# Bucket attention with two feed-forward stages: bucket bits of later pairs in four products per half, and a reordered prologue

## The chip, the cores and the metric

One core of one Trainium2 chip runs the whole program. The metric is the device time of one execution in microseconds (us); lower is better.

## The reference

```python
def _attn_ref(q, k, v, proj):                     # q, k, v: (2, 8, 768, 64), proj: (64, 6)
    q_bits = (np.einsum('bhsd,dk->bhsk', q, proj) > 0).astype(np.int64)
    k_bits = (np.einsum('bhsd,dk->bhsk', k, proj) > 0).astype(np.int64)
    q_bucket = np.sum(q_bits * powers, axis=-1)
    k_bucket = np.sum(k_bits * powers, axis=-1)
    mask = q_bucket[:, :, :, None] == k_bucket[:, :, None, :]
    scores = np.where(mask, scale * np.matmul(q, k.transpose(0, 1, 3, 2)), -1000000000.0)
    scores = scores - np.max(scores, axis=-1, keepdims=True)
    attn = np.exp(scores)
    attn = attn / (np.sum(attn, axis=-1, keepdims=True) + 1e-09)
    return np.matmul(attn, v)
```

The attention's rows (1536 tokens of 512) then go through a mixture of eight experts, of which each token takes one, and through a dense layer with an ELU between two products. The change touches the attention alone.

## The kernel before, in words

There are 16 heads (two batches of eight). Two heads make a **pair**, so there are eight pairs; a head has 768 queries, and 128 of them make a **tile**, so a pair has 12 tiles and the main loop runs over 96 tiles, numbered through. A **half** is 384 of the 768 columns. Every float32 value that goes into a product is split into a rounded part ("hi") and the rest ("lo"), and the products of the parts are added up.

**Operands of the scores.** A head has four arrays: `qa` and `ka` hold hi and lo rows, `qb` and `kb` hold the missing cross term and, from row 64 on, the bucket bits of queries and keys, coded with a huge constant `BIG` so that a pair of different buckets falls far below every other score. There are four sets of these arrays (`st` 0 to 3), two pairs' worth: while one pair is worked on, the next one's are filled.

**Preparing a pair** takes six steps (`prep`, L580): four times `prep_T` (TensorE turns half of the queries or keys, tile `prep`; ScalarE rounds it to hi, VectorE takes lo) and twice `prep_Z` (the bits of a half, tile `zps`). A half of bits is six products in `prep_Zm` (L229): hi, lo and hi again of the queries against rounded weights, the same rounded weights and the weights' rest, then the same for the keys; `prep_Ze` (L245) compares with zero and scales, on VectorE. `restack` (L266) moves the finished rows by DMA from the SP queue to the place where the products want them: six moves of 192 KB for the queries of a pair, six for the keys, six small ones for the bits. In a pair's tiles the steps are issued after tiles 1, 2, 4, 5, 7 and 8, for the next pair.

**A tile** goes through: S (four score products, L314 and L315, into one of two PSUM buffers), M (VectorE's maximum, L333, then two small operations on GpSimd, L334 and L335), E (ScalarE's exponential, L342), T (six transposes, L362, each half rounded by ScalarE, L364, and its rest taken by VectorE, L365), V (four value products per tile, L378) and, for every three tiles, O (the sums of a half, copied by ScalarE, moved by DMA and added by GpSimd, L388) and R (the joining product `sp`, L454, with its two VectorE evictions, L462 and L481). The loop issues tile n's S beside tile n-1's M and E, tile n-3's T and an earlier V. The order on every engine is the order in which the code issues; each engine and the SP queue work strictly in that order. Three PSUM buffers (`ps_t`) serve T, preparation, bits and R.

**The prologue** fills pair 0: its first head's bits are put in place by VectorE without a DMA (`first_Ze`, L238). GpSimd clears constant rows (`constant_rows`), clears and fills `rw` and `rw_end`, the joining weights, and copies a half of the keys. `keep_warm` issues products whose result nobody reads.

Of the kernel before, what the change touches and what calls it, by code (L numbers as in the profile page):

```python
# [8 lines left out]
F32 = mybir.dt.float32  # L9
# [11 lines left out]
NBITS = 6  # L21
# [4 lines left out]
def kernel(  # L26
# [129 lines left out]
        for nm in ("qa", "qb", "ka", "kb"):  # L156
            opnd[st, nm] = ap1.tile([128, S], F32R, name=f"{nm}{st}")

    def constant_rows(st):
        nc.gpsimd.memset(opnd[st, "qb"][64:96].bitcast(F32), 0.0)  # L160
        nc.gpsimd.memset(opnd[st, "qb"][96:96 + NBITS].bitcast(F32), 1.0)
        nc.gpsimd.memset(opnd[st, "kb"][64:96].bitcast(F32), -BIG)

    constant_rows(1)
    bdf, bdh, bdl = (ap1.tile([128, 2, 128], t, name="bd" + x) for x, t in (("f", F32), ("h", F32R), ("l", F32R)))
    nc.vector.memset(bdf, 0.0)
    for hh in range(2):
        rows = slice(64 * hh, 64 * hh + 64)
        src = pj[rows, None, :].to_broadcast([64, 2, NBITS])
        for nm, g0, c0, step in ((0, 32 * hh, 0, NBITS), (1, 64, NBITS * hh, 32)):  # L170
            dst = bdf[rows, nm, g0:g0 + 2 * step].rearrange("p (r c) -> p r c", r=2)[:, :, c0:c0 + NBITS]
            nc.scalar.activation(dst, src, AF.Copy)
    nc.scalar.activation(bdh, bdf, AF.Copy)
    nc.vector.tensor_tensor(bdl, bdf, bdh, ALU.subtract)
    bd = {nm: (bdh[:, i], bdl[:, i]) for i, nm in enumerate("qk")}
    amp = ap1.tile([128, 1], F32, name="amp")
    thr = ap1.tile([128, 1], F32, name="thr")
# [4 lines left out]
        nc.vector.memset(amp[p0:p0 + n], a)  # L182
        nc.vector.memset(thr[p0:p0 + n], t)

    nc.gpsimd.memset(rw, 0.0)
    for hh in range(2):
        p0 = 64 * hh
        rows, idc = slice(p0, p0 + 64), ident[p0:p0 + 64, None, p0:p0 + 64]
        nc.gpsimd.tensor_copy(rw[rows, :, hh, 0:D], idc.to_broadcast([64, H // 2, D]))
        nc.gpsimd.tensor_copy(rw_end[rows, :, 0:D], idc.to_broadcast([64, 2, D]))  # L190
    nc.gpsimd.memset(zt0, 0.0)

    hl = {}

# [52 lines left out]
        )  # L247

    def prep_Z(pr, j):
        prep_Zm(pr, j, "q")  # L250
        prep_Zm(pr, j, "k")

        def evac():
            prep_Ze(pr, j)
            if j == 1 and pr:
                restack(pr, "z")

        return (lambda: None), evac

    def restack(pr, what, heads=(0, 1)):  # L260
        for hh in heads:
            st = 2 * (pr % 2) + hh
            r0 = 64 * hh

            def cp(dst, p0, src, s0, n):
                nc.sync.dma_start(  # L266
                    opnd[st, dst][p0:p0 + n].bitcast(F32), src[s0:s0 + n].bitcast(F32)
                )

            if what == "q":  # L270
                hi, lo = hl[pr, "q"]
                cp("qa", 0, hi, r0, 64)
                cp("qa", 64, lo, r0, 64)
                cp("qb", 0, hi, r0, 64)
            elif what == "k":
                hi, lo = hl[pr, "k"]
                cp("ka", 0, hi, r0, 64)
                cp("ka", 64, hi, r0, 64)
                cp("kb", 0, lo, r0, 64)
            else:  # L280
                cp("kb", 64, zt[pr], (64, 96 + NBITS)[hh], NBITS)
                cp("kb", 96, zt[pr], (96, 64 + NBITS)[hh], NBITS)
                cp("qb", 64, zt[pr], 32 * hh, 2 * NBITS)

    vst = {}

# [103 lines left out]
    def stage_O(m):  # L390
# [2 lines left out]
        r0 = 64 * hh  # L393
        ps = ops.pop(m)
        if pr == NPAIR - 1 or hh == 0:
            t = ap2.tile([128, HC], F32, tag="osb", name="osb", bufs=2)
            osb.setdefault((pr, hf), []).append(t)
        if pr == NPAIR - 1:
            nc.scalar.activation(t, ps, AF.Copy)  # L399
# [2 lines left out]
        if m >= NM - 6:  # L402
            nc.scalar.activation(t, ps[0:64], AF.Copy)
            early.append(lambda: nc.vector.tensor_tensor(t, ps[64:128], t, ALU.add))
        else:
            w, u = (raw_p.tile([128, PW], F32, tag="w", name=x)[:, 0:HC] for x in ("o2", "o1"))
            nc.scalar.activation(w, ps, AF.Copy)
            nc.sync.dma_start(u[r0:r0 + 64], w[64 - r0:128 - r0])
            add.append((3 * m + 11, t, w[r0:r0 + 64], u[r0:r0 + 64]))

    rinv = {}
    sums_m = {}
# [179 lines left out]
    keep_warm(15)  # L592
    for j in range(2):
        both(prep_T(0, "q", j))
    restack(0, "q", (0,))
    for j in range(2):
        both(prep_T(0, "k", j))
    khi, klo = hl[0, "k"]
    nc.scalar.activation(opnd[0, "ka"][0:64], khi[0:64], AF.Copy)
    nc.gpsimd.tensor_copy(opnd[0, "ka"][64:128], khi[0:64])  # L600
    nc.scalar.activation(opnd[0, "kb"][0:64], klo[0:64], AF.Copy)
    for st in (2, 3):
        constant_rows(st)
    for j in range(2):
        prep_Zm(0, j, "q")
    for j in range(2):
# [2 lines left out]
        if j == 0:  # L609
            first_Ze(0, "q", 0, 128)  # L610
    first_Ze(0, "q", 128, HC)
    first_Ze(1, "q")
    load_pair(0, "v")
    load_pair(1, "k")
    for what in ("q", "k"):
        restack(0, what, (1,))

    def load_gates(hh, end):
        rows = slice(64 * hh, 64 * hh + 64)
# [19 lines left out]
    for b in range(B - 1):  # L639
        n0 = per * (b + 1) + HALF + 7  # L640
        for hf in range(2):
# [5 lines left out]
                    at(i, f)  # L647

            at(n0 + 8 * hf, start)
    for j in range(2):  # L650
        at(1, prep_Ze, 0, j)
    at(1, restack, 0, "z", (1,))
    for i in range(6):
        at(1 + i, prep_V, 0, i // 3, i % 3)
    for hh in range(2):
        at(9 + 3 * hh, load_gates, hh, False)
        at(61 + 3 * hh, load_gates, hh, True)
# [225 lines left out]
    for n in range(NQ + 3):  # L883
# [16 lines left out]
            late[0]()  # L900
        if n < NQ:
            stage_S(n)
        m, part = divmod(n - 13, HALF)
        if 0 <= m < NM - 3 and part == 0:
            early.append(stage_R(m))
        if n == NQ:
            stage_R(NM - 3)()
        m, part = divmod(n - 6, HALF)
# [14 lines left out]
            split_piece(0, nc.gpsimd, nc.gpsimd, rest0)  # L923
            xt0 = [raw_p.tile([128, KD * CAP], F32R, tag="w", name="xt0") for _ in range(2)]
        if nx < NPAIR:
            if s % 3 and s < 9:
                late = prep(nx, s // 3 * 2 + s % 3 - 1)
            if s in v_at:
                i = v_at.index(s)
                early.append(lambda a=(nx, i // 3, i % 3): prep_V(*a))  # L930
# [428 lines left out]
```

## Time and profile before

| | |
|---|---|
| median of 3 runs | 722.96 us (722.31 to 724.34) |
| the profiled execution: its time, its span | 723.3 us, 721.5 us |
| mean granted clock of TensorE | 0.993 |
| busy: TensorE / its weight loads | 704.7 us (98%) / 633.3 us (88%) |
| busy: VectorE / ScalarE / GpSimd | 553.6 (77%) / 422.7 (59%) / 206.0 us (29%) |
| attention (tiles 0 to 95) | from about 11 to about 255 us of the span |

Busy time of an engine says where it worked, not what held the others up. The chain that ended last follows the work back from the end, at each step to what released it; the timelines list what an engine did in order, with the idle time before an instruction and what ended it. [...]

### The profile page before, as it was taken

To read this page: it belongs to the slowest core of one execution; us is meant where nothing else is said; L and a number is where in the kernel's file an instruction comes from. 1 tells how busy PE (TensorE), PEld (TensorE's weight loads), DVE (VectorE), ACT (ScalarE), POOL (GpSimd) and SP (SyncE) were. 2 spreads that over 40 slices of the span, in tenths; PEclk is the share of its full clock that TensorE was granted. 3 is DMA by queue.
4 is the path that set the end of the run, shared out by engine and by line. 5 is a ranking of instruction groups with operands and counts; after the bars stand their busy time and mean duration, and the time that the engine had idled before them with its cause. 6 is when DMAs were issued, how large, how long until landed. Compare 5 with 4: busy or idle time off the path is not lost.

```text
span 721.5 us, 12243 instructions
## 1 busy us (share of the span) xinstructions
PE 704.7 (98%) x4239; PEld 633.3 (88%) x4240; DVE 553.6 (77%) x1045; ACT 422.7 (59%) x843; POOL 206.0 (29%) x491
## 2 busy tenths in 40 slices
PE   6999999999999999999999999999999999999996
PEld 4899999999999988999999999788888888888885
DVE  5888988989898988788888887977688546934333
ACT  3887978879788875666666675444543224422221
POOL 7445454455545554112352241000000000002012
PEclk9899999999999999999999999999999999999999
DMA  8747576585773137987889786332122000001011
GB/s 192 181 104 172 163 184 173 129 213 137 167 218 98 76 105 224 291 251 222 260 241 251 203 230 191 103 102 84 63 88 87 31 0 2 1 0 59 0 59 61
DMA packets 108532, 97.69 MB, mean 135 GB/s; under 512 B 33416, under 2 KB 94472, under 8 KB 108464
## 3 DMA queue, kind: packets, MB, share of 16 engines
q1 hardware_dynamic: 106000, 90.44, 46.8%
q0 software_dynamic: 2304, 6.40, 2.4%
q8 instruction: 35, 0.57, 0.3%
q14 instruction: 33, 0.27, 0.1%
q10 hardware_dynamic: 160, 0.00, 0.0%
HBM read 64.15 MB, written 10.72 MB: 104 GB/s over the span
## 4 chain that ended last, share of the span: by engine, by line
PE 52%; issue 32%; DMA 7%; ACT 3%; DVE 2%; POOL 1%; SPq 1%; POOLq 0%; ACTq 0%; DVEq 0%
PE hps L1059 12%; PE o L378 8%; PE yps L1072 8%; PE t L362 7%; DMA out_dram<-part,tidt 5%; PE s L314 4%; PE s L315 4%; PE yps L1074 3%; PE zps L229 2%; PE sp L454 2%; ACT p L342 1%; PE prep L203 1%; PE xTp L1041 1%; DMA qb<-qhi 1%; DVE ptlo L365 1%
## 5 line engine op out<-in xcount | busy, mean ns | idle before, releaser
L365 DVE TENSOR_TENSOR ptlo<-t,pthi 128x384 fp32r<-128x384 f32 x192 | 100.1, 549 | 26.7 <-ACT pthi L364 24.5
L342 ACT ACTIVATE p<-s,bi,sc 128x768 f32<-128x768 f32 x96 | 96.1, 1001 | 21.4 <-POOL bi L335 20.0
L364 ACT ACTIVATE pthi<-t 128x384 fp32r<-128x384 f32 x192 | 84.9, 498 | 24.6 <-PE t L362 23.7
L765 DVE TENSOR_TENSOR wl<-wraw,wh 128x1024 fp32r<-128x1024 f32 x63 | 77.3, 1229 | 21.8 <-ACT wh L762 19.6
L333 DVE TENSOR_REDUCE nm<-s 128x1 f32<-128x768 f32 x96 | 91.0, 948 | 0.3 <-POOL vst L293 0.3
L1211 POOL DMA_INDIRECT out_dram<-part,tidt x12 | 11.5, 962 | 263.5 <-DVE part L1208 262.2
L1173 ACT ACTIVATE ee<-gps 128x512 f32<-128x512 f32 x48 | 28.7, 599 | 97.9 <-PE gps L1163 97.9
L1072 PE MATMUL yps<-h,wh 128*128 128x448 f32 x256 | 84.4, 380 | 0.0
L362 PE MATMUL t<-ident,p 128*128 128x128 f32 x576 | 80.5, 275 | 1.6 <-DVE qlo L212 1.6
L314 PE MATMUL s<-ka,qa 128*128 128x384 f32 x192 | 74.3, 387 | 3.0 <-ACT p L342 2.6
L1163 PE MATMUL gps<-x2h,vl 128*128 128x512 f32 x192 | 75.9, 395 | 0.0
L1193 PE MATMUL a<-vh,gh 128*128 128x512 f32 x192 | 75.6, 394 | 0.0
L1193 PE MATMUL a<-vh,gl 128*128 128x512 f32 x192 | 75.4, 393 | 0.0
L1163 PE MATMUL gps<-x2h,vh 128*128 128x512 f32 x192 | 75.3, 392 | 0.0
L1163 PE MATMUL gps<-x2l,vh 128*128 128x512 f32 x192 | 75.2, 392 | 0.0
L1193 PE MATMUL a<-vl,gh 128*128 128x512 f32 x192 | 74.9, 390 | 0.0
L362 PEld LDWEIGHTS t<-ident,p 128*128 128x128 f32 x576 | 68.5, 142 | 5.2 <-DVE qlo L212 2.0
L1174 DVE TENSOR_SCALAR ee<-ee 128x512 f32<-128x512 f32 x48 | 20.4, 425 | 66.2 <-ACT ee L1173 66.2
L1176 ACT ACTIVATE gh<-ee 128x512 fp32r<-128x512 f32 x48 | 30.4, 634 | 69.2 <-DVE ee L1175 69.2
L378 PE MATMUL o<-pthi,vst 128*128 128x384 f32 x192 | 67.1, 349 | 0.8 <-ACT osb L399 0.6
L315 PE MATMUL s<-kb,qb 102*128 102x384 f32 x192 | 66.2, 345 | 0.8 <-DMA qb<-qhi 0.8
L762 ACT ACTIVATE wh<-wraw 128x1024 fp32r<-128x1024 f32 x63 | 66.1, 1052 | 0.2 <-DMA wraw<-in_moe_w_dram 0.2
(204 smaller groups left out, 1772.1 us busy)
## 6 DMA issues: line engine op xcount, KB each, us to landing
wraw<-in_moe_w_dram SPq DMA_DIRECT2D x64, 512.0 KB
w<-in_moe_w_in_dram SPq DMA_DIRECT2D x16, 512.0 KB
w<-in_moe_w_out_dram SPq DMA_DIRECT2D x16, 512.0 KB
ka<-khi SPq DMA_DIRECT2D x30, 192.0 KB
xs_d<-zt SPq DMA_DIRECT2D x8, 528.0 KB
xs<-xs_d SPq DMA_DIRECT2D x8, 528.0 KB
raw_q<-in_q_dram SPq DMA_DIRECT2D x16, 192.0 KB
raw_k<-in_k_dram SPq DMA_DIRECT2D x16, 192.0 KB
```

Source lines behind the costliest of these rows:

```text
L314: nc.tensor.matmul(ps[:, j, 0:HC], opnd[st, "qa"][:, cb], opnd[st, "ka"][:, sl], start=True, stop=False)
L315: nc.tensor.matmul(ps[:, j, 0:HC], opnd[st, "qb"][0:64 + MROWS, cb], opnd[st, "kb"][0:64 + MROWS, sl], start=False, stop=True,)
L333: nc.vector.tensor_reduce(nm, sps[n][:, :, 0:HC], AX.XY, ALU.max, negate=True)
L342: nc.scalar.activation(p.rearrange("p (a b) -> p a b", a=2), sps.pop(n)[:, :, 0:HC], AF.Exp, bias=bi, scale=sc, accum_out=sums[hd][:, c:c ...
L362: nc.tensor.transpose(ps[:, a, :], p[:, kt * 128:(kt + 1) * 128], ident)
L364: nc.scalar.activation(ho, ps, AF.Copy)
L365: nc.vector.tensor_tensor(lo[:, HALF * g:HALF * (g + 1), i * 128:(i + 1) * 128], ps, ho, ALU.subtract)
L378: nc.tensor.matmul(ops[m], vst[hd][:, kt, :], t[:, kt, :], start=(kt == 0 and x == 0), stop=(kt == NC - 1 and x == 1))
L1059: nc.tensor.matmul(ps, w[:, dc, fs], x[:, dc], start=(i == 0), stop=(i == len(terms) - 1))
L1072: nc.tensor.matmul(ps, wh[:, f], h[:, :, f], start=(f == 0), stop=last)
L1163: nc.tensor.matmul(ps, w[:, dc], x[:, dc, th * TC:(th + 1) * TC], start=(dc == 0 and i == 0), stop=(dc == KD - 1 and i == 2),)
L1193: nc.tensor.matmul(ps, x[:, cs], w, start=(fb in first_fb and i == 0), stop=(fb in last_fb and i == 2))
```

## The change

For pairs 1 to 7 the bits of a half take four products: the weights' hi and lo stand side by side in one 128-column array `zw`, so hi and lo of the queries, then of the keys, each go once through it, and the four products add up. Columns 64 to 127 hold the weights' rest with the sign turned; ScalarE copies that half of the result out, VectorE asks whether the other half is greater, and GpSimd scales the answer by `zamp`, in place, before the bits are moved. This work is issued in the next tile right after the maximum. R comes two tiles later up to pair 5, and so does GpSimd's addition; `osb` has three buffers.

In the prologue the first half of head 0's query rows is copied by GpSimd, and the other half moved by DMA; the second half's query bits are placed by VectorE after the first two maxima; head 1's rows are moved earlier; constants of later sets, the `rw_end` copies and one clearing go into the first tiles or ahead; pair 1 is prepared after tiles 3 to 8; and eight products without a reader follow tile 1's scores.

```diff
--- before.py
+++ after.py
@@ -156,14 +156,23 @@
         for nm in ("qa", "qb", "ka", "kb"):
             opnd[st, nm] = ap1.tile([128, S], F32R, name=f"{nm}{st}")
 
-    def constant_rows(st):
-        nc.gpsimd.memset(opnd[st, "qb"][64:96].bitcast(F32), 0.0)
-        nc.gpsimd.memset(opnd[st, "qb"][96:96 + NBITS].bitcast(F32), 1.0)
-        nc.gpsimd.memset(opnd[st, "kb"][64:96].bitcast(F32), -BIG)
+    def constant_rows(st, parts=range(3)):
+        for i in parts:
+            nm, p0, n, a = (("qb", 64, 32, 0.0), ("qb", 96, NBITS, 1.0), ("kb", 64, 32, -BIG))[i]
+            nc.gpsimd.memset(opnd[st, nm][p0:p0 + n].bitcast(F32), a)
 
     constant_rows(1)
-    bdf, bdh, bdl = (ap1.tile([128, 2, 128], t, name="bd" + x) for x, t in (("f", F32), ("h", F32R), ("l", F32R)))
+    constant_rows(2)
+    bdf, zwf = (
+        raw_p.tile([128, PW], F32, tag="w", name=x)[:, 0:2 * n].rearrange("p (i c) -> p i c", i=2)
+        for x, n in (("bdf", 128), ("zwf", 64))
+    )
+    bdh, bdl, zw = (ap1.tile([128, 2, 128], F32R, name=x) for x in ("bdh", "bdl", "zw"))
+    zamp = ap1.tile([64, 1], F32, name="zamp")
     nc.vector.memset(bdf, 0.0)
+    nc.vector.memset(zwf, 0.0)
+    for p0, n, a in ((0, 32, 1.0), (32, 32, -BIG), (32, 2 * NBITS, 2.0 * BIG)):
+        nc.vector.memset(zamp[p0:p0 + n], a)
     for hh in range(2):
         rows = slice(64 * hh, 64 * hh + 64)
         src = pj[rows, None, :].to_broadcast([64, 2, NBITS])
@@ -172,6 +181,12 @@
             nc.scalar.activation(dst, src, AF.Copy)
     nc.scalar.activation(bdh, bdf, AF.Copy)
     nc.vector.tensor_tensor(bdl, bdf, bdh, ALU.subtract)
+    for hh in range(2):
+        rows = slice(64 * hh, 64 * hh + 64)
+        src = pj[rows, None, :].to_broadcast([64, 2, NBITS])
+        for i, c0, step in ((0, 2 * NBITS * hh, NBITS), (1, 32 + NBITS * hh, 2 * NBITS)):
+            dst = zwf[rows, i, c0:c0 + 2 * step].rearrange("p (r c) -> p r c", r=2)[:, :, 0:NBITS]
+            nc.scalar.activation(dst, src, AF.Copy)
     bd = {nm: (bdh[:, i], bdl[:, i]) for i, nm in enumerate("qk")}
     amp = ap1.tile([128, 1], F32, name="amp")
     thr = ap1.tile([128, 1], F32, name="thr")
@@ -182,13 +197,15 @@
         nc.vector.memset(amp[p0:p0 + n], a)
         nc.vector.memset(thr[p0:p0 + n], t)
 
-    nc.gpsimd.memset(rw, 0.0)
-    for hh in range(2):
+    nc.gpsimd.tensor_copy(zw[:, :, 0:64], zwf)
+    nc.gpsimd.tensor_tensor(zw[:, :, 64:128], zw[:, :, 0:64], zwf, ALU.subtract)
+    def joining_rows(t, hh):
         p0 = 64 * hh
         rows, idc = slice(p0, p0 + 64), ident[p0:p0 + 64, None, p0:p0 + 64]
-        nc.gpsimd.tensor_copy(rw[rows, :, hh, 0:D], idc.to_broadcast([64, H // 2, D]))
-        nc.gpsimd.tensor_copy(rw_end[rows, :, 0:D], idc.to_broadcast([64, 2, D]))
-    nc.gpsimd.memset(zt0, 0.0)
+        if t is rw:
+            nc.gpsimd.tensor_copy(rw[rows, :, hh, 0:D], idc.to_broadcast([64, H // 2, D]))
+        else:
+            nc.gpsimd.tensor_copy(rw_end[rows, :, 0:D], idc.to_broadcast([64, 2, D]))
 
     hl = {}
 
@@ -247,15 +264,25 @@
         )
 
     def prep_Z(pr, j):
-        prep_Zm(pr, j, "q")
-        prep_Zm(pr, j, "k")
+        sl = slice(j * HC, (j + 1) * HC)
+        if j == 0:
+            zt[pr] = ap2.tile([128, S], F32R, tag="z", name="z", bufs=1)
+        ps = ps_t.tile([128, HC], F32, tag="t", name="zps")
+        for i, nm in enumerate("qk"):
+            for x, t in enumerate(hl[pr, nm]):
+                nc.tensor.matmul(ps, zw[:, i], t[:, sl], start=(i == 0 and x == 0), stop=(i == 1 and x == 1))
+        low = zt[pr][64:128, sl].bitcast(F32)
+        nc.scalar.activation(low, ps[64:128], AF.Copy)
+        z = zt[pr][0:64, sl]
 
         def evac():
-            prep_Ze(pr, j)
-            if j == 1 and pr:
+            nc.vector.tensor_tensor(z, ps[0:64], low, ALU.is_gt)
+            nc.gpsimd.tensor_scalar(z, z, zamp, None, ALU.mult)
+            if j == 1:
                 restack(pr, "z")
 
-        return (lambda: None), evac
+        early.append(evac)
+        return []
 
     def restack(pr, what, heads=(0, 1)):
         for hh in heads:
@@ -278,9 +305,10 @@
                 cp("ka", 64, hi, r0, 64)
                 cp("kb", 0, lo, r0, 64)
             else:
-                cp("kb", 64, zt[pr], (64, 96 + NBITS)[hh], NBITS)
-                cp("kb", 96, zt[pr], (96, 64 + NBITS)[hh], NBITS)
-                cp("qb", 64, zt[pr], 32 * hh, 2 * NBITS)
+                k0, k1, q0 = (32 + NBITS * hh, 32 + NBITS * (2 + hh), 2 * NBITS * hh) if pr else (96 + NBITS, 64 + NBITS, 32)
+                cp("kb", 64, zt[pr], k0, NBITS)
+                cp("kb", 96, zt[pr], k1, NBITS)
+                cp("qb", 64, zt[pr], q0, 2 * NBITS)
 
     vst = {}
 
@@ -393,7 +421,7 @@
         r0 = 64 * hh
         ps = ops.pop(m)
         if pr == NPAIR - 1 or hh == 0:
-            t = ap2.tile([128, HC], F32, tag="osb", name="osb", bufs=2)
+            t = ap2.tile([128, HC], F32, tag="osb", name="osb", bufs=3)
             osb.setdefault((pr, hf), []).append(t)
         if pr == NPAIR - 1:
             nc.scalar.activation(t, ps, AF.Copy)
@@ -406,7 +434,7 @@
             w, u = (raw_p.tile([128, PW], F32, tag="w", name=x)[:, 0:HC] for x in ("o2", "o1"))
             nc.scalar.activation(w, ps, AF.Copy)
             nc.sync.dma_start(u[r0:r0 + 64], w[64 - r0:128 - r0])
-            add.append((3 * m + 11, t, w[r0:r0 + 64], u[r0:r0 + 64]))
+            add.append((3 * m + (13 if m < NM - 8 else 11), t, w[r0:r0 + 64], u[r0:r0 + 64]))
 
     rinv = {}
     sums_m = {}
@@ -592,15 +620,22 @@
     keep_warm(15)
     for j in range(2):
         both(prep_T(0, "q", j))
-    restack(0, "q", (0,))
+    (qhi, qlo), first = hl[0, "q"], slice(0, HC)
+    nc.gpsimd.tensor_copy(opnd[0, "qa"][0:64, first], qhi[0:64, first])
+    nc.gpsimd.tensor_copy(opnd[0, "qa"][64:128, first], qlo[0:64, first])
+    nc.gpsimd.tensor_copy(opnd[0, "qb"][0:64, first], qhi[0:64, first])
+    for nm, p0, t in (("qa", 0, qhi), ("qa", 64, qlo), ("qb", 0, qhi)):
+        nc.sync.dma_start(opnd[0, nm][p0:p0 + 64, HC:].bitcast(F32), t[0:64, HC:].bitcast(F32))
     for j in range(2):
         both(prep_T(0, "k", j))
     khi, klo = hl[0, "k"]
     nc.scalar.activation(opnd[0, "ka"][0:64], khi[0:64], AF.Copy)
     nc.gpsimd.tensor_copy(opnd[0, "ka"][64:128], khi[0:64])
     nc.scalar.activation(opnd[0, "kb"][0:64], klo[0:64], AF.Copy)
-    for st in (2, 3):
-        constant_rows(st)
+    nc.gpsimd.memset(rw, 0.0)
+    for hh in range(2):
+        joining_rows(rw, hh)
+    constant_rows(3, (0, 1))
     for j in range(2):
         prep_Zm(0, j, "q")
     for j in range(2):
@@ -609,11 +644,10 @@
         if j == 0:
             first_Ze(0, "q", 0, 128)
     first_Ze(0, "q", 128, HC)
-    first_Ze(1, "q")
+    restack(0, "q", (1,))
     load_pair(0, "v")
+    restack(0, "k", (1,))
     load_pair(1, "k")
-    for what in ("q", "k"):
-        restack(0, what, (1,))
 
     def load_gates(hh, end):
         rows = slice(64 * hh, 64 * hh + 64)
@@ -647,11 +681,17 @@
                     at(i, f)
 
             at(n0 + 8 * hf, start)
+    at(1, keep_warm, 8)
+    at(1, lambda: early.append(lambda: first_Ze(1, "q")))
     for j in range(2):
-        at(1, prep_Ze, 0, j)
-    at(1, restack, 0, "z", (1,))
+        at(2 + j, prep_Ze, 0, j)
+    at(3, restack, 0, "z", (1,))
     for i in range(6):
-        at(1 + i, prep_V, 0, i // 3, i % 3)
+        at(2 + i, prep_V, 0, i // 3, i % 3)
+    at(5, constant_rows, 3, (2,))
+    for hh in range(2):
+        at(8 + hh, joining_rows, rw_end, hh)
+    at(10, nc.gpsimd.memset, zt0, 0.0)
     for hh in range(2):
         at(9 + 3 * hh, load_gates, hh, False)
         at(61 + 3 * hh, load_gates, hh, True)
@@ -900,9 +940,9 @@
             late[0]()
         if n < NQ:
             stage_S(n)
-        m, part = divmod(n - 13, HALF)
-        if 0 <= m < NM - 3 and part == 0:
-            early.append(stage_R(m))
+        for m in range(NM - 3):
+            if n == 3 * m + (15 if m < NM - 8 else 13):
+                early.append(stage_R(m))
         if n == NQ:
             stage_R(NM - 3)()
         m, part = divmod(n - 6, HALF)
@@ -923,8 +963,9 @@
             split_piece(0, nc.gpsimd, nc.gpsimd, rest0)
             xt0 = [raw_p.tile([128, KD * CAP], F32R, tag="w", name="xt0") for _ in range(2)]
         if nx < NPAIR:
-            if s % 3 and s < 9:
-                late = prep(nx, s // 3 * 2 + s % 3 - 1)
+            i = s - 3 if pr == 0 else s // 3 * 2 + s % 3 - 1 if s % 3 else -1
+            if 0 <= i < 6:
+                late = prep(nx, i)
             if s in v_at:
                 i = v_at.index(s)
                 early.append(lambda a=(nx, i // 3, i % 3): prep_V(*a))
```

**TensorE, pair 1, end of tile 19 (`sp` and `o`, then the bits) and the transposes of the next tile.** Before:

```order
L454 MATMUL sp<-rw,osb 128x160 x3
L378 MATMUL o<-pthi,vst 128x384
L378 MATMUL o<-ptlo,vst 128x384
L378 MATMUL o<-pthi,vst 128x384
L378 MATMUL o<-ptlo,vst 128x384
L229 MATMUL zps<-qhi,bdh 128x384
L229 MATMUL zps<-qlo,bdh 128x384
L229 MATMUL zps<-qhi,bdl 128x384
L229 MATMUL zps<-khi,bdh 128x384
L229 MATMUL zps<-klo,bdh 128x384
L229 MATMUL zps<-khi,bdl 128x384
L362 MATMUL t<-ident,p 128x128 x6
```

and now:

```order
L406 MATMUL o<-pthi,vst 128x384
L406 MATMUL o<-ptlo,vst 128x384
L406 MATMUL o<-pthi,vst 128x384
L406 MATMUL o<-ptlo,vst 128x384
L273 MATMUL zps<-qhi,zw 128x384
L273 MATMUL zps<-qlo,zw 128x384
L273 MATMUL zps<-khi,zw 128x384
L273 MATMUL zps<-klo,zw 128x384
L390 MATMUL t<-ident,p 128x128 x6
```

Two of the six bit products are gone, and `sp` stands two tiles further down; it now follows the scores of tile 21.

**VectorE, tiles 0 to 3 of the prologue (`nm` is the maximum, `qb` and `z` the bits, `ptlo` the evictions of T).** Before:

```order
L238 TENSOR_SCALAR qb_125<-zps,thr,amp 38x256
L238 TENSOR_SCALAR qb_125<-zps,thr,amp 38x384
L333 TENSOR_REDUCE nm<-s 128x1
L245 TENSOR_SCALAR z<-zps,amp 128x384 x2
L333 TENSOR_REDUCE nm<-s 128x1
L212 SCALAR_TENSOR_TENSOR qlo<-prep,qhi 128x384
L333 TENSOR_REDUCE nm<-s 128x1
L365 TENSOR_TENSOR ptlo<-t,pthi 128x3x128 x2
```

and now:

```order
L255 TENSOR_SCALAR qb_125<-zps,thr,amp 38x256
L361 TENSOR_REDUCE nm<-s 128x1 x2
L255 TENSOR_SCALAR qb_125<-zps,thr,amp 38x384
L262 TENSOR_SCALAR z<-zps,amp 128x384
L361 TENSOR_REDUCE nm<-s 128x1
L393 TENSOR_TENSOR ptlo<-t,pthi 128x3x128 x2
L262 TENSOR_SCALAR z<-zps,amp 128x384
L361 TENSOR_REDUCE nm<-s 128x1
```

Both first maxima come ahead of the second half's bits, and the first preparation's `qlo` has left this stretch.

**The SP queue, moves for pair 1 (sets 2 and 3) in pair 0.** Before:

```order
L266 DMA qb_137<-qhi 64x768
L266 DMA ka_134<-khi 64x768 x2
L266 DMA kb_135<-klo 64x768
L266 DMA ka_138<-khi 64x768 x2
L266 DMA kb_139<-klo 64x768
L132 DMA raw_q<-in_q_dram 128x6x64 x2
L132 DMA raw_k<-in_k_dram 128x6x64 x2
L408 DMA o_562<-o_561 64x384
L266 DMA kb_135<-z 6x768 x2
```

and now:

```order
L293 DMA qb_137<-qhi 64x768
L132 DMA raw_q<-in_q_dram 128x6x64 x2
L132 DMA raw_k<-in_k_dram 128x6x64 x2
L293 DMA ka_134<-khi 64x768 x2
L293 DMA kb_135<-klo 64x768
L293 DMA ka_138<-khi 64x768 x2
L293 DMA kb_139<-klo 64x768
L436 DMA o_586<-o_585 64x384
L293 DMA kb_135<-z 6x768 x2
```

The loads of pair 2's queries and keys stand ahead of the moves of pair 1's keys, where they stood behind them; the bits' moves are still last.

## Rows read from the trace of the kernel before

**Rows 1.** Windows view, 160 to 180 us: length; busy us (instructions) per engine; granted clock; DMA share; GB/s

```profile
160.00:180.00 20.00, 19.99 (x138) 19.34 (x137) 18.68 (x39) 17.64 (x42) 10.07 (x32) 1.00 0.56 138
```

**Rows 2.** Chain that ended last, whole span: start us, us, piece

```profile
60.50 0.82 PE sp L454 x6
61.32 0.70 PE o L378 x4
62.02 1.04 PE zps L229 x6
63.06 0.66 PE t L362 x6
...
215.15 1.04 PE zps L229 x6
```

**Rows 3.** Chain that ended last, asked to 60 us, tiles 13 and 14

```profile
46.90 0.33 PE prep L203 x3
...
47.88 0.18 PE s L314
```

**Rows 4.** Chain that ended last, asked from 150 to 215 us

```profile
178.21 0.97 ACT p L342 x2
```

**Rows 5.** Timeline of PE: start, us, instruction [idle before <- releaser]

```profile
16.36 0.45 PE L314 MATMUL s<-ka,qa 128*128 128x384 f32 x1 [2.26 <-ACT p L342]
...
19.62 0.90 PE L362 MATMUL t<-ident,p 128*128 128x128 f32 x3 [1.63 <-DVE qlo L212]
...
43.17 0.42 PE L314 MATMUL s<-ka,qa 128*128 128x384 f32 x1
```

**Rows 6.** Windows view of two single microseconds of the prologue

```profile
18.00:19.00 1.00, 0.00 (x0) 0.00 (x0) 0.00 (x0) 0.52 (x2) 0.00 (x0) 0.60 1.06 249
25.00:26.00 1.00, 1.00 (x10) 1.00 (x9) 0.44 (x2) 0.55 (x2) 0.83 (x4) 0.98 0.90 227
```

**Rows 7.** Timeline of DVE, prologue

```profile
13.53 0.96 DVE L333 TENSOR_REDUCE nm<-s 128x1 f32<-128x768 f32 x1
...
15.46 0.95 DVE L333 TENSOR_REDUCE nm<-s 128x1 f32<-128x768 f32 x1
```

**Rows 8.** Timeline of ACT, prologue

```profile
15.22 0.99 ACT L342 ACTIVATE p<-s,bi,sc 128x768 f32<-128x768 f32 x1 [4.71 <-POOL bi L335]
...
18.48 0.49 ACT L208 ACTIVATE qhi<-prep 128x384 fp32r<-128x384 f32 x1 [2.18 <-DMA qb<-qhi]
18.87 0.99 ACT L342 ACTIVATE p<-s,bi,sc 128x768 f32<-128x768 f32 x1
```

**Rows 9.** Timeline of SP (its DMA issues), pair 0

```profile
29.06 1.10 SPq L266 DMA_DIRECT2D ka<-khi  x2
...
33.24 2.12 SPq L132 DMA_DIRECT2D raw_q<-in_q_dram  x2
35.46 1.40 SPq L132 DMA_DIRECT2D raw_k<-in_k_dram  x2
...
40.04 0.74 SPq L266 DMA_DIRECT2D qb<-z  x1
```

**Rows 10.** Groups by line and form, whole span: shapes xcount | busy us, mean ns | idle before

```profile
L388 POOL TENSOR_TENSOR osb<-o,o 64x384 f32<-64x384 f32 x26 | 26.3, 1010 | 0.9
...
L245 DVE TENSOR_SCALAR z<-zps,amp 128x384 fp32r<-128x384 f32 x16 | 9.7, 609 | 0.0
...
L404 DVE TENSOR_TENSOR osb<-o,osb 64x384 f32<-64x384 f32 x2 | 1.1, 560 | 0.8 <-ACT osb L403 0.8
...
L403 ACT ACTIVATE osb<-o 64x384 f32<-64x384 f32 x2 | 1.0, 483 | 0.0
...
L600 POOL CAST ka<-khi 64x768 fp32r<-64x768 f32 x1 | 0.8, 821 | 1.5 <-ACT khi L208 1.5
```

**Rows 11.** Timeline of SP, pair 1

```profile
70.25 0.74 SPq L266 DMA_DIRECT2D qb<-z  x1
```

**Rows 12.** Timeline of PE, tile 24, the first of pair 2

```profile
73.61 0.42 PE L314 MATMUL s<-ka,qa 128*128 128x384 f32 x1
```

## The prediction

> **What bounds the kernel now.** I read the windows view first. In a stretch of the attention TensorE is busy 19.99 of 20 us, VectorE 18.68 and ScalarE 17.64 [rows 1]: TensorE leads, but the other two are close behind. Then the chain that ended last. In the middle of the attention it runs from one TensorE piece to the next [rows 2]; only in some stretches does it pass through an exponential of ScalarE and what lies around it [rows 4]. The piece of the bits of a half, six products, takes 1.04 us there, the value products of a tile 0.70, the transposes 0.66, R 0.82 [rows 2]; a score product takes 0.18 and a preparation's transposes 0.33 [rows 3].
>
> From these a pair's TensorE work adds up: twelve tiles of 0.66 + 4 x 0.18 + 0.70 = 2.08 make 25.0 us, four preparations 1.3, two halves of bits 2.1, R twice 1.6: 30.0 us. The same piece of bits stands at 62.02 and, five pairs later, at 215.15 [rows 2], so a pair takes 30.63 us. Of these TensorE lacks work for some 0.6 us. A product that goes from a pair therefore shortens it, as long as the 0.6 doesn't grow.
>
> The prologue is another matter. There I read the timelines engine by engine. TensorE idles 2.26 us before tile 2's scores at 16.36 and 1.63 us before the second half of tile 0's transposes at 19.62 [rows 5]; its granted clock has fallen to 0.5 within the microsecond from 18 on (mean 0.60), and is back at 1.0 within the one from 25 on (mean 0.98) [rows 6]. Tile 12, the first of pair 1, has its scores at 43.17 [rows 5]. Why the idle times: the first maximum starts at 13.53, the second only at 15.46, with bits between them [rows 7]. The first exponential comes 1.69 us after its maximum's start, at 15.22; the second at 18.87, because ScalarE stood for 2.18 us before a `qhi` of pair 1 that waited for the move of head 1's queries out of the same buffer [rows 8].
>
> **The change part by part.**
>
> *Four products for six.* Of 1.04 us for six products [rows 2] two are 0.35 us per half. Pairs 1 to 7 have 14 halves. Pair 1's two lie in the prologue's stretch and are counted there; twelve remain: 12 x 0.35 = 4.2 us, all of it on the path.
>
> *What takes their place.* ScalarE copies 64 x 384 (0.48 us, as the copy of that shape), VectorE compares 64 x 384 (0.56 us as that shape's addition, for 0.61 before) and GpSimd scales 64 x 384 in place; for that the trace has no row: an addition of two such inputs takes 1.01 us, a cast of one input of twice the length 0.82, so 0.41 to 1.01 [rows 10]. I take 0.41, one input being the nearer case. These hide: ScalarE has 2.4 us free in 20 and gains twice 0.48 in 30 [rows 1, 10], and GpSimd works half the time [rows 1]. Without that cover they would cost 1 us a pair. Behind the GpSimd step wait the next tile's `sc` and `bi`, a tile later, so they have room; the SP queue waits for it too. Before, the last move of pair 2's bits was issued at 70.25 and took 0.74 to issue, and tile 24's scores began at 73.61 without a wait, their first product with the bits one product (0.2) later [rows 3, 11, 12]. That leaves 2.8 us for landing and slack. The new path is longer by 0.48 + 0.41 to 1.01 and shorter by the two evictions it is moved ahead of, so I count nothing.
>
> *R and GpSimd's addition two tiles later.* R leaves the tile that also carries a half's bits; no work is removed. It could give back part of the 0.6 us a pair or nothing. I take nothing and keep the upper end, 0.6 x 6 = 3.8 us, for the range.
>
> *The prologue.* The first maximum moves ahead of a bits step of VectorE and so comes about 0.6 earlier, the price of such a step [rows 10]; its exponential then starts at about 14.6 and tile 2's scores, 1.14 after that as now [rows 5, 8], at 15.8. The second maximum follows the first at once, and its exponential at 15.6 in place of 18.87. So tile 3's scores follow tile 0's transposes directly, at 15.8 + 0.72 + 0.66 = 17.2. The eight products without a reader fill TensorE's wait before tile 2 at about 0.18 each, the score product's price [rows 3]: 1.4 us inside a wait of about 2, so they cost nothing, and I take it that the clock stays up. GpSimd's three copies of 64 x 384 (0.41 each by [rows 10]) replace moves by DMA; I count on them to end before VectorE has the first bits, so that scores start when they did, and if they don't they cost up to 1.2 us. The four new copies for `zw` on ScalarE lie beside the loads of the first queries. GpSimd's other displaced work (a clearing in tile 5, two copies in 8 and 9, a clearing in 10) goes into an engine that is half idle [rows 1], as do the moves of head 1's rows, now ahead of pair 1's keys, which nobody wants before tile 5. Then four tiles at 2.4 (2.08 + 0.33) bring tile 7 to 26.8, two with bits at 2.08 + 0.69 tile 9 to 32.3, three at 2.08 tile 12 to 38.6: 4.6 us before the 43.17 of now.
>
> *What is late next: the SP queue.* Pair 1 is prepared two tiles or more later, and pair 2's loads now stand ahead of the keys' moves. By the steps above tile 5's scores come at 22.0 and tile 6's at 24.4; the second half of pair 1's `qlo` is VectorE's last step between them, about 23.8. From there the queue has six query moves (4.2 us, as the six of the keys, 29.06 to 33.24), the loads (33.24 to 36.86: 3.6), the keys' moves (4.2), then the move of O's sums and the first head's bits (36.86 to 40.78: 3.9) [rows 9]: 39.7. How long the last one takes to land no row says: at least nothing, and at most the 2.6 us from 40.78 to tile 12's product with the bits at 43.4, one product after its first, which did not wait [rows 5, 9]. I take 1.2, the middle: 40.9, where that product would have come at 38.8. That eats 2.1 of the 4.6, and the prologue brings 2.5 us (3.7 with the one end, 1.1 with the other). [...]
>
> **Sum.** 4.2 + 2.5 = 6.7 us. The profiled execution took 723.3 us, 1.8 more than its span and 0.3 more than the median of 722.96; 722.96 - 6.7 gives 716.3. What follows the attention is only moved forward: its weights come in later tiles by the same tile numbers.
>
> **The rivals.**
>
> *The clock falls again in the prologue.* For it: between tile 3 and tile 6 TensorE will still wait for evictions. Against: the two long waits [rows 5] are the ones that the change shortens or fills. Then of the prologue only the first 0.6 us are left, and 4.2 + 0.6 leads to 718.2. [...]
>
> *ScalarE and VectorE become the bound.* For it: 18.68 and 17.64 of 20 us [rows 1] and a chain that passes through exponentials [rows 4]; ScalarE gets another 1 us a pair. Against: VectorE loses a little, and both had waits in the tiles with bits. If the 4.2 us all turn into waits, 2.5 are left: 720.5; if half, 718.4.
>
> *Spreading R pays too.* The upper end of that step, 3.8 us on top, gives 712.5.
>
> *Slower: the bits come late in every pair.* Place: the first tile of each pair, whose score product waits for the bits' moves, now behind ScalarE, VectorE, GpSimd and SP in turn. The spare 2.8 us there shrink by the 0.35 saved on TensorE and by landing. To end 2.2 us above the median, six pairs must lose 6.7 + 2.2 = 8.9, or 1.5 us each, so the new path must be some 3 us longer than the old one, and I count at most 1.5 - 0.9. Nothing on GpSimd's or SP's timeline gives that; the time would be about 725.2.
>
> **How the numbers follow.** Forecast, 0.60: 716.3, with 714 to 718 for the landing and the prologue's steps. Clock falls, 0.12. Bound shifts, 0.14. Spreading pays, 0.10. Bits late, 0.04. The range 712.5 to 720.3 takes in all but the last and the worst of the third. A measurement of this kernel tells about 0.3% (2.2 us) from no change; so faster is below 720.8: all but the last case, and most of the third, 0.90; same 0.06, slower 0.04.
>
> **What would show it.** In the profile after: pieces of four products of about 0.69 us; pairs some 0.7 us shorter, 29.9; a granted clock of 1.0 in every microsecond from 10 to 30; the second exponential near 15.6; tile 12's scores near 40.7, with a wait of its bit product for a move of `z`. I am wrong if pairs keep 30.6 us with waits of TensorE for ScalarE, if the clock shows 0.5 before 30 us, or if first tiles of later pairs wait for a DMA.

## The result, and the profile after

| | |
|---|---|
| median of 6 runs after / before | 730.42 us (729.20 to 732.22) / 722.96 us (722.31 to 724.34) |
| ratio, 95% interval | 1.0106 (1.0092 to 1.0119) |
| profiled execution after: time, span, clock | 729.82 us, 728.1 us, 0.996 |

The change made the kernel 7.5 us slower where 6.7 us less were forecast. The starts of the exponentials show where. Tile 12 is 2.85 us earlier than before (43.42 for 46.27), tile 24 2.28 earlier, tile 72 1.47 later, tile 84 5.75 later, tile 94 5.55 later. So the prologue gained, each later pair lost, and pair 7's first tile lost 4.3 us at once.

**The prologue** gained what was forecast. ScalarE's timeline has the first two exponentials at 14.17 and 15.15, where before they started at 15.22 and 18.87 [rows 8]:

```profile
14.17 0.99 ACT L370 ACTIVATE p<-s,bi,sc 128x768 f32<-128x768 f32 x1 [4.11 <-POOL bi L363]
...
15.15 0.98 ACT L370 ACTIVATE p<-s,bi,sc 128x768 f32<-128x768 f32 x1
```

The windows (TensorE, its loads, VectorE, ScalarE, GpSimd busy; granted clock as a share of full speed; DMA) show the clock at 1.0 where it had fallen [rows 6] (it is 1.00 in every microsecond from 10 to 30), and TensorE short of work in the middle of the attention, 19.38 busy us in 20 for 19.99 [rows 1]:

```profile
160.00:180.00 20.00, 19.38 (x131) 18.36 (x130) 17.43 (x37) 16.43 (x37) 10.63 (x34) 1.00 0.50 124
18.00:19.00 1.00, 1.00 (x8) 0.63 (x7) 1.00 (x3) 1.00 (x3) 0.54 (x2) 1.00 1.34 234
```

Tile 12's product with the bits waits for their move and starts at 40.83; the last move of that head's bits is issued on SP's queue at 38.08 (first row). One piece of bits is now four products in 0.70 us for six in 1.04 [rows 2]. The timelines of SP's queue and TensorE:

```profile
38.08 0.74 SPq L293 DMA_DIRECT2D qb<-z  x1
...
40.83 0.41 PE L343 MATMUL s<-kb,qb 102*128 102x384 f32 x1 [0.90 <-DMA kb<-z]
...
58.88 0.34 PE L273 MATMUL zps<-qhi,zw 128*128 128x384 f32 x1
59.05 0.34 PE L273 MATMUL zps<-qlo,zw 128*128 128x384 f32 x1
59.23 0.33 PE L273 MATMUL zps<-khi,zw 128*128 128x384 f32 x1
59.40 0.33 PE L273 MATMUL zps<-klo,zw 128*128 128x384 f32 x1
```

**A pair** takes 31.55 us after, 30.62 before (the time between the starts of the exponentials of tiles 24 and 72, divided by four). The timelines of VectorE (one row, the maximum of tile 31) and GpSimd in tiles 7 and 8 of pair 2:

```profile
89.81 0.95 DVE L361 TENSOR_REDUCE nm<-s 128x1 f32<-128x768 f32 x1
...
89.44 0.19 POOL L363 TENSOR_TENSOR bi<-sc,nm 128x1 f32<-128x1 f32 x1
89.70 1.01 POOL L416 TENSOR_TENSOR osb<-o,o 64x384 f32<-64x384 f32 x1
90.78 0.29 POOL L320 CAST vst<-raw_v 128x128 fp32r<-128x128 f32 x1
91.16 0.46 POOL L321 TENSOR_TENSOR vst<-raw_v,vst 128x128 fp32r<-128x128 f32 x1
91.70 0.23 POOL L445 TENSOR_SCALAR sm<-sums 128x3 f32<-128x3 f32 x1
92.01 0.22 POOL L362 TENSOR_SCALAR sc<-nm 128x1 f32<-128x1 f32 x1
92.32 0.19 POOL L363 TENSOR_TENSOR bi<-sc,nm 128x1 f32<-128x1 f32 x1
92.82 1.26 POOL L280 TENSOR_SCALAR z<-z,zamp 64x384 fp32r<-64x384 f32 x1 [0.32 <-DMA ka<-khi]
94.05 0.20 POOL L362 TENSOR_SCALAR sc<-nm 128x1 f32<-128x1 f32 x1
```

The moved addition stands in one tile with a value cast (0.75 for its two steps) and the row sums, and tile 31's scale and bias of the exponential (`sc`, `bi`) come after all of them: the maximum has ended at 90.76, `sc` starts at 92.01, 1.25 us later. Before, the addition stood behind `sc` and `bi`, and `sc` of the same tile started 0.08 us after its maximum had ended (92.42):

```profile
91.47 0.95 DVE L333 TENSOR_REDUCE nm<-s 128x1 f32<-128x768 f32 x1
...
92.13 0.23 POOL L417 TENSOR_SCALAR sm<-sums 128x3 f32<-128x3 f32 x1
92.50 0.23 POOL L334 TENSOR_SCALAR sc<-nm 128x1 f32<-128x1 f32 x1
92.81 0.19 POOL L335 TENSOR_TENSOR bi<-sc,nm 128x1 f32<-128x1 f32 x1
93.08 1.01 POOL L388 TENSOR_TENSOR osb<-o,o 64x384 f32<-64x384 f32 x1
```

On TensorE's timeline after the change R's first products in that pair wait for VectorE's compare of the bits, and later scores for an exponential:

```profile
95.24 1.05 PE L482 MATMUL sp<-rw,osb 128*128 128x160 f32 x6 [0.37 <-DVE z L279]
...
102.12 0.44 PE L342 MATMUL s<-ka,qa 128*128 128x384 f32 x1 [0.33 <-ACT p L370]
```

**Tile 84.** Two rows of GpSimd's timeline, the additions:

```profile
216.28 1.01 POOL L416 TENSOR_TENSOR osb<-o,o 64x384 f32<-64x384 f32 x1
...
224.40 1.02 POOL L416 TENSOR_TENSOR osb<-o,o 64x384 f32<-64x384 f32 x1
```

SP's queue in that stretch:

```profile
217.31 0.37 SPq L107 DMA_DIRECT2D wraw<-in_moe_w_dram  x1
...
221.85 0.88 SPq L293 DMA_DIRECT2D kb<-klo  x1
225.44 0.46 SPq L436 DMA_DIRECT2D o<-o  x1
225.95 0.59 SPq L107 DMA_DIRECT2D wraw<-in_moe_w_dram  x1
226.58 1.52 SPq L293 DMA_DIRECT2D kb<-z  x2
```

The weight piece at 217.31 and O's move at 225.44 each start 0.02 us after an addition has ended (216.28 + 1.01, 224.40 + 1.02). Pieces and O's two copies share six buffers (`raw_p`); an addition two tiles later gives its two back two tiles later. The moves of pair 7's bits stand behind both in the queue. Before, O's move and the first of the bits' ran there at

```profile
218.85 0.46 SPq L408 DMA_DIRECT2D o<-o  x1
...
221.77 1.52 SPq L266 DMA_DIRECT2D kb<-z  x2
```

and the bits' now come 4.81 us later. TensorE's timeline then has a wait of 1.85 us within tile 84:

```profile
231.01 0.66 PE L343 MATMUL s<-kb,qb 102*128 102x384 f32 x1 [1.85 <-DMA qb<-z]
```

and behind it, in the three microseconds from 231 to 234, the clock is at 0.50 (third column from the right; one of them):

```profile
232.00:233.00 1.00, 1.00 (x5) 1.00 (x5) 0.65 (x1) 0.00 (x0) 0.00 (x0) 0.50 0.44 105
```

### The profile page after: what moved, and what is told of

Read it like the earlier page. It is cut to its first block, busy times and chain, and to the rows that moved or that the text cites. A ratio compares the mean times of both kernels' runs of the same rounds, so it can differ in the third digit from the quotient of the medians.

```text
span 728.1 us, 12263 instructions
## 1 busy us (share of the span) xinstructions
PE 706.3 (97%) x4219; PEld 628.2 (86%) x4220; DVE 556.8 (76%) x1049; ACT 428.7 (59%) x861; POOL 221.3 (30%) x510
## 4 chain that ended last, share of the span: by engine, by line
issue 35%; PE 34%; DMA 8%; ACT 7%; POOL 7%; DVE 7%; SPq 2%; POOLq 0%; DVEq 0%; ACTq 0%
PE hps L1100 10%; PE yps L1113 7%; DMA out_dram<-part,tidt 4%; PE yps L1115 3%; PE o L406 3%; ACT p L370 3%; PE t L390 2%; ACT pthi L392 2%; DVE nm L361 2%; DVE ptlo L393 2%; POOL osb L416 2%; PE s L342 1%; PE sp L482 1%; PE s L343 1%; SPq L293 1%
```

## The experiments

The suspects: GpSimd's scaling of the bits, 1257 ns each (S); the two tiles' delay of R and of the additions (D). Each group of runs had runs of the kernel before beside it (medians 723.9 to 724.8, 1 to 2 us above the 722.96 from which the expectations start), so ratios to those are compared. "Pair" is the length as above, "tile 12" and "tile 94" the start of that exponential against before's 46.27 and 254.07 (minus: earlier).

| kernel | ratio (95%) | median us | pair | tile 12 | tile 94 |
|---|---|---|---|---|---|
| the change | 1.0106 (1.0092-1.0119) | 730.42 | 31.55 | -2.85 | +5.55 |
| e1 sums back | 0.9947 (0.9929-0.9966) | 720.40 | 30.02 | -2.65 | -5.73 |
| e2 scaling on VectorE | 1.0147 (1.0123-1.0172) | 735.58 | 31.97 | -2.36 | +10.37 |
| e3 both | 0.9979 (0.9963-0.9995) | 722.48 | 30.08 | -2.85 | -2.65 |
| e4 prologue only | 1.0015 (1.0002-1.0028) | 725.28 | 30.58 | -3.14 | -0.22 |
| e5 four products only | 0.9948 (0.9925-0.9972) | 719.42 | 29.92 | -1.96 | -5.84 |
| e6 additions back | 0.9938 (0.9914-0.9962) | 719.09 | 30.14 | -2.73 | -5.70 |
| e7 shorter delay | 1.0030 (1.0016-1.0044) | 726.35 | 31.24 | -2.59 | +0.03 |
| e8 e4, GpSimd shifted | 0.9972 (0.9957-0.9987) | 721.91 | 30.60 | -2.25 | -1.95 |
| e9 e7, casts moved | 0.9973 (0.9958-0.9987) | 722.22 | 30.10 | +0.98 | -2.19 |
| e10 e5 and filler | 0.9952 (0.9934-0.9971) | 719.69 | 30.00 | -1.77 | -5.20 |
| e11 e1, extra additions | 0.9969 (0.9955-0.9982) | 721.84 | 30.18 | -2.15 | -3.66 |
| e12 e6, extra additions | 1.0022 (1.0007-1.0037) | 725.02 | 31.04 | -2.40 | -0.21 |

### e1, e2, e3: delay or scaling

e1, with two `osb` buffers again:

```diff
-            if n == 3 * m + (15 if m < NM - 8 else 13):
+            if n == 3 * m + 13:
-            add.append((3 * m + (13 if m < NM - 8 else 11), t, ...
+            add.append((3 * m + 11, t, ...
```

> The changed kernel with the joining of sums (R) and GpSimd's addition of O's halves put back to their tiles of before (3m+13, 3m+11, two output buffers instead of three); all else as changed. Theory S, GpSimd's scaling of the bits (1.26 us each, ahead of the next tile's sc and bi) makes pairs longer, and the move of the additions only makes the wait of pair 7's first tile, because it keeps two of the six buffers that weight pieces also use: pairs stay at 31.4 us, the 4.2 us at tile 84 go, about 726. Theory D, the delay itself makes both: pairs of 30 us, about 717. If neither: 730, tile 84 waits as before.

e2 (e3 is e1 and e2 together):

```diff
-            nc.gpsimd.tensor_scalar(z, z, zamp, None, ALU.mult)
+            nc.vector.tensor_scalar(z, z, zamp, None, ALU.mult)
```

> The changed kernel with the scaling of the bits on VectorE behind its compare, in place of GpSimd; R and the additions stay two tiles later. Theory S: pairs fall from 31.4 to about 30.0 us, six of them 8 us, and tile 84 still waits for the moves of its bits: about 722. Theory D: at most 1 us better, 729 to 730. If VectorE has become the bound, slower than 730.

> Both edits together: scaling on VectorE, R and the additions at their tiles of before. If S and D between them are the whole loss, the prediction's own sum comes out: 716 to 718, pairs of 30.0 us, no wait for a DMA at tile 84. If the third suspect carries it (ScalarE's copy of the bits, for which VectorE's compare waits), pairs stay at 30.6 or more and the time at 720 to 722.

D holds and S falls. Without the delay pairs take 30.02 us and tile 84 does not wait; the scaling may stand on GpSimd (e1) or VectorE (e3), pairs are the same. With the delay VectorE's scaling makes it worse (e2). e1 ends at 720.40 where theory D had about 717, and e3 misses its 716 to 718: it loses 2.7 us between tiles 84 and 94, behind a wait of GpSimd (2.12 us) that e4 has too (2.24).

### e4, e8: the prologue alone

e4 is the kernel after with six products and one eviction for every pair and e1's edit. e8 adds:

```diff
+    for i in range(14):
+        at(13 + i, spacer)
```

> The prologue and pair 1's later preparation as changed, but six products per half with VectorE's single step for every pair, and R and the additions at their tiles of before. If the prologue keeps what it showed at tile 12 (2.9 us there): 720 to 721, pairs of 30.6 us. If that gain is lost again further on, 722 to 723.

> The prologue alone (as e4) with fourteen one-element clears added to GpSimd's list, one a tile in tiles 13 to 26; they compute nothing that is used. In e4 GpSimd stands 2.24 us before its first scatter, its 377th instruction, for nothing that the profile shows, and the exponential behind it is late; with 390 instructions ahead of it (e1, the change) it stood 0.30. If that wait belongs to a position in the list: 0.3 us before the scatter and 2 us less, 0.998 of before or better. If not: the wait stays and the time is e4's.

e4 (725.28, above both of its ranges) keeps 3.0 us up to tile 84 and loses 2.8 behind it. GpSimd's timeline has 2.24 us of idle time before its first scatter of token rows:

```profile
227.19 0.24 POOL L435 TENSOR_SCALAR sm<-sums 128x3 f32<-128x3 f32 x1
229.66 1.21 POOL L582 DMA_INDIRECT xs_d<-xw,g_idx  x1 [2.24 <-issue]
```

and ScalarE stands 2.31 us before the next exponential, TensorE 1.95 before the next scores. The granted clock is lower there too, 0.50 in the microsecond from 235; how much of the loss is the clock's was not measured:

```profile
235.00:236.00 1.00, 1.00 (x6) 0.91 (x5) 0.68 (x1) 0.00 (x0) 0.16 (x1) 0.50 0.39 139
```

On e8's timeline, with fourteen tiny clears more in the list, that instruction waits 0.39, and tile 94 keeps its 1.95 us:

```profile
228.85 1.21 POOL L582 DMA_INDIRECT xs_d<-xw,g_idx  x1 [0.39 <-issue]
```

So by itself the prologue is worth some 2.0 us (0.9972 of 724.29), and e4's loss is a wait that hangs on the place in GpSimd's list.

### e5, e10: the four products alone

e5 is the kernel before with `prep_Z`, `zw`, `zamp` and the bits' moves of the change. e10 adds `at(1, keep_warm, 8)`.

> The kernel before, its prologue included, with the four products, ScalarE's copy, VectorE's compare and GpSimd's scaling for pairs 1 to 7, and their weights made in the setup; nothing else. If the steady term of the prediction holds where R and the additions stand as before: pairs of 30.1 us for 30.6, 0.993 to 0.995 of the time before. If the gain seen in e1 against e4 needs the new prologue: no difference from before.

> The kernel of e5 (four products, prologue as before) with the eight products without a reader in tile 1 alone. If the clock's fall in the prologue is what the filler spares: granted clock 1.0 in every microsecond from 16 to 26 where e5 has 3.5 us at 0.5, some 1.7 us less than e5. If the wait before tile 2 is too long to fill: the clock falls later or as before, and the time is e5's.

The steady term holds with the old prologue: 0.9948, 3.8 us, pairs 0.70 shorter. In the trace the old prologue also does better here: tile 12 is 1.96 earlier, and e5's clock is at 0.50 in the three microseconds from 19 to 22 and 0.86 in the next, where before fell in that from 18 and was back in that from 25 [rows 6]. Why it comes back sooner there stays open. The trace is of the fastest of seven runs (718.45 us, mean clock 0.997); the three slowest took 721.35 to 722.70 at 0.991 to 0.993, so the 1.96 us need not hold for all. The filler alone does not spare the fall. Windows of e10, from 19 to 23:

```profile
19.00:20.00 1.00, 0.46 (x2) 0.46 (x3) 1.00 (x2) 1.00 (x3) 0.00 (x0) 0.75 0.94 204
20.00:21.00 1.00, 1.00 (x6) 1.00 (x5) 0.84 (x2) 0.77 (x3) 0.48 (x3) 0.50 1.00 280
21.00:22.00 1.00, 1.00 (x6) 0.90 (x5) 1.00 (x3) 1.00 (x2) 0.62 (x2) 0.50 0.10 20
22.00:23.00 1.00, 1.00 (x6) 1.00 (x5) 0.97 (x3) 0.81 (x3) 0.00 (x0) 0.54 0.46 104
```

0.75, 0.50, 0.50 and 0.54 are about 3.4 us at half clock, as in e5 and 0.6 us later, and the time is e5's within the intervals.

### e6, e7, e9: what of the delay

e6 has only the second half of e1's diff. e7:

```diff
-            if n == 3 * m + (15 if m < NM - 8 else 13):
+            if n == 3 * m + (15 if m < NM - 14 else 13):
-            add.append((3 * m + (13 if m < NM - 8 else 11), t, ...
+            add.append((3 * m + (13 if m < NM - 14 else 11), t, ...
```

e9 is e7 with

```diff
-    v_at = (3, 5, 6, 8, 9, 11)
+    v_at = (2, 4, 5, 8, 10, 11)
```

> The changed kernel with GpSimd's addition of O's halves back at 3m+11; R stays at 3m+15. Theory A, the addition's new tiles carry the loss (it stands behind the value casts and the row sums there, R's products wait for it, and VectorE's maxima behind R's evictions): pairs of 30.1 us, R's products without waits for GpSimd, no wait at tile 84 since the move buffers come free as before, 720 to 722. Theory P, R's own new place carries it (its PSUM piece waits for VectorE's compare of the bits): pairs stay near 31.3 us, 726 or more.

> The changed kernel with the two tiles' delay of R and the additions ended six half-heads earlier (m below 18 and not 24), so that no half-head holds its two move buffers longer while weight pieces are loaded. If the wait of tile 84 is these buffers: it goes, the other pairs keep 31.3 us, about 725 to 726. If the wait comes from anything else in the order of SP's queue: 730 as before this edit.

> The kernel of e7 (delay kept, but not while weight pieces are loaded) with GpSimd's casts of the values taken out of the tiles that now have the addition: they run in tiles 3, 5, 6, 9, 11 and 0 of a pair for 4, 6, 7, 9, 10 and 0. Theory L, the delayed additions cost because GpSimd's list of tiles 4, 7 and 10 (scale and bias of the exponential, addition 1.0, casts 0.75, row sums 0.24) became longer than the tile: most of what e7 loses against e6 comes back, 719 to 722. Theory W, R's products come too close behind an addition that is two tiles ahead of them, or the buffers held longer cost: e7's 726 stays.

e6: with the additions back the whole loss is gone; R two tiles later costs nothing by itself. e7: the wait of tile 84 is the six buffers' (e6, where R stays late, has no such wait either). SP's queue there runs again as before, O's move at 219.14 and the bits' at 221.59:

```profile
219.14 0.46 SPq L436 DMA_DIRECT2D o<-o  x1
219.64 0.87 SPq L107 DMA_DIRECT2D wraw<-in_moe_w_dram  x1
221.59 1.52 SPq L293 DMA_DIRECT2D kb<-z  x2
```

e9: with the casts out of those tiles, the additions where the change put them and R as close behind them, pairs take 30.10 us for e7's 31.24. GpSimd's timeline there shows idle time again before a scale:

```profile
91.64 1.01 POOL L416 TENSOR_TENSOR osb<-o,o 64x384 f32<-64x384 f32 x1
92.73 0.24 POOL L445 TENSOR_SCALAR sm<-sums 128x3 f32<-128x3 f32 x1
93.05 0.21 POOL L362 TENSOR_SCALAR sc<-nm 128x1 f32<-128x1 f32 x1
93.34 0.19 POOL L363 TENSOR_TENSOR bi<-sc,nm 128x1 f32<-128x1 f32 x1
93.90 1.26 POOL L280 TENSOR_SCALAR z<-z,zamp 64x384 fp32r<-64x384 f32 x1 [0.37 <-DVE z L279]
95.86 0.21 POOL L362 TENSOR_SCALAR sc<-nm 128x1 f32<-128x1 f32 x1 [0.70 <-DVE nm L361]
```

e9 loses in pair 0, where tile 12 is 0.98 later than before. There a cast that was moved ahead waits for its values to be loaded, `sc` and `bi` stand behind it, and TensorE's scores behind those; then the clock is at 0.50 in every microsecond from 24 to 30.

```profile
21.50 0.29 POOL L320 CAST vst<-raw_v 128x128 fp32r<-128x128 f32 x1 [3.41 <-DMA raw_v<-in_v_dram]
...
24.71 0.69 PE L342 MATMUL s<-ka,qa 128*128 128x384 f32 x1 [2.88 <-ACT p L370]
```

### e11, e12: the load by itself

Both add in `stage_A`, after the additions, on e1 and on e6 (e12 writes two dead weight tiles):

```diff
+        if n % 3 == 1 and 13 <= n < 85:
+            src = ident[0:64, None, :].to_broadcast([64, 3, 128])
+            nc.gpsimd.tensor_tensor(extra, src, src, ALU.add)
```

> The kernel of e1 (R and the additions where they stood before) with one more GpSimd addition of 64 x 384 in each tile that the change moved additions to (tile numbers 1 modulo 3, from 13 to 82), of constants into a tile that nothing reads. Theory L: pairs go from 30.1 to 31.0 us or more as in the change, without R or any buffer moved: 725 to 727. Theory W: GpSimd is half idle, so 720 as e1.

> The kernel of e6 (R two tiles later, GpSimd's additions at their tiles of before) with e11's extra load: GpSimd additions of constants, 64 x 256 and 64 x 128, into weights that are dead after the prologue, in the tiles numbered 1 modulo 3 from 13 to 82. e11 lost only 0.16 us a pair by that load with R at its old tiles. If the load and R's later place together make the change's loss: pairs of 31 us or more, 726. If the load costs as little here (30.3 us a pair, 721), it is the moved addition itself that something waits for.

A load of that size costs 0.16 us a pair with R at its old tiles (0.82 us each, e11) and 0.90 with R two tiles later (1.0 us each, e12). So theory L was half right: the full list costs little alone. Beside the later R it costs most of what the change lost.

The timelines show how. Take the tiles 4, 7 and 10 of pairs 2 to 5 and two means for each: how late `sc` starts after its maximum has ended, and the slack, from the end of `bi` to the start of the exponential, which then waits for something else. `sc` is 0.08 to 0.17 us late in e1 and e6. The load makes it about equally late in both kernels: 0.77, 0.91 and 0.94 in e11, 0.91, 0.91 and 0.66 in e12 (so the somewhat larger load of e12 is not the difference). But the slack that takes this up is 0.76, 1.20 and 0.55 us in e1, and with the later R only 0.51, 0.64 and 0.04 in e6. What the added lateness exceeds the slack by comes to these sums a pair:

| | e11 | e12 | the change | e9 |
|---|---|---|---|---|
| lateness beyond the slack, us a pair | 0.36 | 1.05 | 1.55 | 0.05 |
| pairs longer than in e1 (e11) or e6 (the others) | 0.16 | 0.90 | 1.41 | -0.04 |

What of the later R shortens the slack is argued, not shown: R's evictions on VectorE and its GpSimd step `lg` fall into the tiles of the load then.

## Why the prediction was wrong

**The prologue: right, its exact number by luck.** The clock stayed up (1.00 in every microsecond from 10 to 30); 2.5 us were forecast, tile 12 was 2.85 earlier, and e8 measures 2.0 alone. The bit product of tile 12 was forecast for 40.9 and came at 40.83, but by misses that cancel: the first head's moves were issued by 38.82 (38.08 + 0.74) and not 39.7, from there to the product are 2.0 us and not 1.2, and TensorE was ready for it at about 39.9 (40.83 less its wait of 0.90) and not 38.8. The gain hardly adds to that of the four products: e1 and e5 end alike (0.9947, 0.9948), in part because e5's trace gains 1.96 by tile 12 without it.

**The four products: right.** 0.35 us a half was forecast; pairs are 0.6 to 0.7 shorter in e1, e5 and e10. Beside the 4.2 us stands what the traces gain from tile 12 to tile 94: 3.9 in e5, 3.4 in e10, 3.1 in e1, 3.0 in e6. (That e5's median also gains 3.8 is chance: its prologue's gain is in it, and so is what it loses behind the attention.)

**GpSimd's scaling: mis-sized, and not the cause.** "For that the trace has no row" was wrong: the kernel before scales token rows by one factor per partition in its expert stage, and that form stands among the groups by shape of the trace before:

```profile
L787 POOL TENSOR_SCALAR xs<-xs 128x512 f32<-128x512 f32 x14 | 32.1, 2302 | 100.6 <-PE hps L1059 63.2 <-DMA xs<-xs_d 37.4
```

2.3 us for 512 columns make some 1.7 for 384, an estimate; it measured 1.26, above both ends taken (0.41 to 1.01). What it hid behind held, though: e1 pays nothing for it.

**R and GpSimd's addition two tiles later: the step that failed.** "No work is removed; I take nothing and keep the upper end" left the other sign out. The change against e6 is that step's addition alone: 1.0106 for 0.9938, 1.7% or some 12 us. Two prices were to be read. First, what GpSimd has to do in the tile that the addition goes to (three of four also have a cast): cast 0.75, sums 0.24, `sc` and `bi` 0.4, and now 1.01: 2.4 us, in tiles of 2.1 to 2.8; "half idle" was an average over tiles. By itself such a list costs 0.16 us a pair (e11); it costs 0.90 and more because the same step, by moving R, also takes away the slack of the exponential behind it (e12). Second, what is held until the addition has run: two of six buffers that the weight pieces also take, and a queue in which the last pair's bits stand behind both. That cost 4.3 us at tile 84, the fall of the clock behind the wait (0.50 from 231 to 234) included; in e7 neither is there: tile 84's exponential starts 2.30 us after tile 83's, in the change 6.19.

**The rivals.** ScalarE and VectorE did not become the bound: with e6 they do the same work in pairs of 30.14 us. "Spreading R pays" fell (e6 against e1, intervals overlap). "Bits come late" happened in one pair, by a buffer, not by the longer path of the bits that was priced there.

e6 beats both kernels, at 0.9938 of before; e1, e5 and e10 can't be told from it. Without the failed step the change is thus worth 4.5 us, 2.2 less than the 6.7: in e6's trace the prologue gives 2.7, the tiles from 12 to 94 3.0 for 4.2, and 0.9 of these 5.7 is lost by the end of the span (4.8). In e1, e8 and e11 TensorE waits once for 1.4 us in the expert stage for GpSimd's scaled rows, which is part of what they give back there.

## What to carry to other kernels

A step that moves is priced like one that is added: count, tile by tile, what its engine already does where it goes, not the engine's mean share, and how late the work behind it may come before something waits. Then list what the step holds until it has run (buffers, places in a queue) and who else draws on the same pool. An operation without a row of its own shape often has one elsewhere in the same trace; look at all rows of its form before bounding it by other forms.

## What the hardware showed that was not expected

- GpSimd's scaling by one factor per partition took longer in the change than an addition of two inputs of that size: 1.26 us for 64 x 384 (L280) against 1.01 (L416); an addition whose inputs are a repeated row block took 0.82 (e11).
- GpSimd stood 2.12 and 2.24 us before its first scatter in e3 and e4, where its timeline lists 375 instructions ahead of it, and 0.30 to 0.39 before it with 370 (before), 386 (e5, e10), 389 (the change, e1, e6 to e9), 413 (e11) and 437 (e12). (e8's expectation counts one more each.) e2 has 375 too, but there GpSimd had just waited 3.7 us for a maximum, so it decides nothing. e8, with fourteen more in the list, stood 0.39 us for e4's 2.24: the place in the list matters; why is open.
